# Block 1 of a fused attention and SwiGLU kernel: t's weight blocks made ahead of the weights' own, the last two pairs' steps moved into the down phase, silu queued behind the copy of P7

## The chip, the core and the metric

The kernel runs on one core of a Trainium2 chip. The metric is device time in microseconds (us), the median of several executions. A core has five engines with a queue of their own each, and each works through its queue in order: PE (TensorE, matrix products; PEld is its weight load), DVE (VectorE), ACT (ScalarE), POOL (GpSimd), and SP (SyncE), which here only issues DMA transfers. PE writes into PSUM banks; DVE and ACT read them and write SBUF; POOL works on SBUF alone.

## The reference

All in float32: linear attention with an RMS norm for 8 batches of 576 tokens and 8 heads of 64, then a SwiGLU feed-forward over 4608 tokens of width 512 with an inner width of 1536.

```python
kv = np.einsum('bhsd,bhse->bhde', k, v)
out = np.einsum('bhsd,bhde->bhse', q, kv)
rms = np.sqrt(np.mean(out * out, axis=-1, keepdims=True) + 1e-06)
x = (out / rms * g_norm)            # -> (4608, 512)
...
g = x @ w_gate
silu = g * (1.0 / (1.0 + np.exp(-g)))
val = x @ w_val
return silu * val @ w_out
```

## The kernel before

The 4608 tokens are nine blocks of 512, `blocks[0]` to `blocks[8]`. For each block n an `Ffn` object runs an *up* phase (gate and value products, silu, their product into the tile h) and a *down* phase (h times w_out). While block n is in its down phase, the attention of block n+1 is done in between: `Att.steps` gives three pieces of work that `down` runs after its products P1, P6 and P2 (query times kv and the norm of the first half; the same for the second half; the rest with `sums`).

Matrix products are done with seven block products in place of eight (Winograd's form of Strassen's method), named P1 to P7 by the number p in `multiply(p)`. Three PSUM banks carry the chains: b takes P1, P6, P7 and P4 one after the other; a takes P2; c takes P5 and then P3. After each product a method `after1` to `after7` takes what stands in the bank: ACT copies b after P1 (line 567), P6 (line 571) and P7 (line 601), DVE adds a after P2 (line 597) and c after P7 (line 603) and P3 (line 611). A product that adds to a bank must wait until the former contents have been read: P4 waits for the copy of P7, P3 for the add of c at line 603, P6 for the copy of P1. The DVE and POOL operations show in the profile with the lines of three helpers: add is L111, sub is L112, mul is L113.

Block 0 uses plain products. Block 1 uses one level of the seven-product form (class `Up`): six units, one for each pair j of 128-wide column groups; a unit holds pair j of w_gate and of w_val as a 2 x 2 block matrix. Blocks 2 to 8 (`DEEP` = 2) use two levels (class `Inner`), for which the second-level weight blocks, the *leaves*, have to exist. They are made once, in block 1, from the weights that its products have just used:

- For each unit, POOL makes three tiles t (for P5, P7 and P4) in `prepare`, one unit ahead, from a pool of nine.
- `leaf_steps` yields the making of leaves as small functions: for each operand two in-place steps on DVE, two more DVE subtractions into a room, and sends of the results to DRAM tiles w0 to w2 on SP's queue. For t's operands the room is a tile r and there are two sends (w<-t and w<-r). For the weights' own operands (o = 1, 2 in w_gate and 6, 3 in w_val) the room is the tile xi (`leaf_room`, one for all pairs), with one send (w<-xi) for w_gate and one for w_val; the rest stays in place.
- `Up.multiply` puts these steps into the list `making` after P5, P7 and P4 (t's) and after P3 (the weights' own); `make(4)` runs four after each product of the up phase, `make(12)` twelve after each of the down phase.

Unit i runs in the order P1, P5, then P4 and P3 of unit i-1, then P6, P2, P7 (`sequence`). P4 and P3 of a pair therefore lie in the next pair's unit. After P4, ACT applies silu to one half and POOL multiplies it into h (line 608); after P3 DVE adds c and POOL multiplies again (line 612), and DVE's `h_sums` reads and changes that part of h. After P7, before this change, ACT's queue holds the silu of s (line 602, on the sum that line 597 made on DVE) and then the copy of P7 (line 601).

The down phase of block 1 runs P1, P5, P6, P7, P2, P4, P3. Its t tiles are made by POOL from w_out (`turn_t`; t<-wo in the profile). Block 2 fetches its leaves from DRAM on SP's queue through the same nine t tiles (`Stream.pump`, t<-w in the profile), and its `sums` write a tile xi from the same single buffer as `leaf_room`. On SP, block 1 also holds loads of k and v (lines 263), of q for block 2 (line 300), and of q for block 3 in 32 small pieces (line 280).

A scheduler orders each engine's instructions at build time by the order in the program and by its own estimate of when each can start; `tc.issue_after(ins)` keeps what is traced inside it behind `ins` where both are on the same engine, without a wait of its own between engines.

Of the kernel before, what the change touches and what calls it, by code (L numbers as in the profile page):

```python
# [12 lines left out]
ACT = mybir.ActivationFunctionType  # L13
# [5 lines left out]
def kernel(  # L19
# [41 lines left out]
    nc = tc.nc  # L61
# [11 lines left out]
    NP = NF // 2  # L73
# [34 lines left out]
    wg, wv = ([consts.tile([P, NS, 2 * P], F32, name=f"{x}{j}") for j in range(NP)] for x in ("wg", "wv"))  # L108
# [6 lines left out]
    def ring():  # L115

        return r_pool.tile([P, 4, BLK], F32, name="r")

    class Words:
# [12 lines left out]
        def __init__(self, src, shape):  # L132
            self.raw = ld_pool.tile([P, LD], U32, name="ld")[:, 0 : 2 * BLK]
            dst = self.raw.rearrange("p (a b) -> p a b", a=shape[0])
            self.sent = nc.sync.dma_start(out=dst, in_=src)
            self.shape = shape
            self.begun = False
# [392 lines left out]
    class Quad:  # L530
# [11 lines left out]
        def multiply(self, p):  # L542
            name, first = CHAIN[p]
            if first:
                tiles = [PSUMS[name].tile([P, 2, HB], F32, name=name) for _ in range(1 + (name in self.apart))]
                self.ps[name], self.apart[name] = tiles[0], tiles[-1]
            banks = self.ps[name], self.apart[name]
            for e, i in self.order(p):
                lhsT, rhs = self.operands(p, e, i)

                nc.tensor.matmul(  # L551
                    banks[e][:, e], lhsT=lhsT, rhs=rhs, start=first and i == 0 and (e == 0 or banks[0] is not banks[1]),
                    stop=i == self.steps - 1, skip_group_check=True,
                )
            getattr(self, f"after{p}", lambda: None)()
# [17 lines left out]
    class Up(Quad):  # L573
# [24 lines left out]

        def after7(self):
            self.u3 = self.piece(2)  # L600
            nc.scalar.copy(out=self.u3, in_=self.ps["b"])
            nc.scalar.activation(out=self.s, in_=self.s, func=ACT.Silu)
            add(nc.vector, self.u3, self.ps["c"], self.u3)

        def after4(self):
# [9 lines left out]
        def multiply(self, p):  # L615
            super().multiply(p)
            ffn = self.ffn
            if ffn.n != DEEP - 1:
                return

            if p == 5:
                self.leaf_room = ring().rearrange("p f (s c) -> p (f s) c", c=P)
            if p in (5, 7, 4):
                at = 3 * (5, 7, 4).index(p)
                ffn.making.extend(leaf_steps(self.j, [(self.w[p].unsqueeze(1), (p,))], self.leaf_room[:, at:]))
            if p == 3:
                if ffn.leaf_room is None:
                    ffn.leaf_room = x_pool.tile([P, 3, 7, P], F32, name="xi").rearrange("p a b c -> p (a b) c")
                halves = lambda t: t[self.j].rearrange("p (o i) c -> p o i c", o=2)
                ffn.making.extend(leaf_steps(self.j, [(halves(wg), (1, 2)), (halves(wv), (6, 3))], ffn.leaf_room))  # L630

    class Inner:

# [167 lines left out]
    def leaf_steps(j, sources, room):  # L801


        d, f = divmod(j, 2)
        i = 0

        def send(leaf, count, src):
            at = LEAVES.index(leaf)
            tc.keep_in_program_order(nc.sync.dma_start(out=stream.dram[d][:, at : at + count, f], in_=src))

        for t, os in sources:
            n = len(os)
            t = t.rearrange("p o i (e c) -> p o i e c", e=2)
            b11, t2_, b22 = t[:, :, 0, 0], t[:, :, 0, 1], t[:, :, 1, 1]
            to = room[:, i : i + 3 * n].rearrange("p (o r) c -> p o r c", r=3)
            yield lambda b22=b22, t2_=t2_: sub(nc.vector, t2_, b22, t2_)
            yield lambda b11=b11, t2_=t2_: add(nc.vector, t2_, t2_, b11)
            yield lambda t=t, t2_=t2_, to=to, n=n: sub(
                nc.vector, to[:, :, 0:3:2], t[:, :, 1], t2_.unsqueeze(2).to_broadcast([P, n, 2, P])
            )  # L820
            if os[0] not in RESIDENT:
                yield lambda t=t, o=os[0]: send((o, 1), 4, t[:, 0].rearrange("p i e c -> p (i e) c"))
            yield lambda b11=b11, t2_=t2_, to=to: sub(nc.vector, to[:, :, 1], b11, t2_)
            yield lambda i=i, n=n, o=os[0]: send((o, 4), 3 * n, room[:, i : i + 3 * n])
            i += 3 * n
# [88 lines left out]
    class Ffn:  # L914
        def __init__(self, n, att):
            self.n, self.att = n, att
            self.h = h_pool.tile([P, NF, BLK], F32, name="h")
            self.ps, self.making, self.leaf_room, self.ended = {}, [], None, None

        def store(self, o, t, columns=slice(None)):  # L920
            rows = out[BLK * self.n : BLK * (self.n + 1), columns].rearrange("(t p) d -> p t d", t=T)
# [8 lines left out]
            return sub(engine, a21, s1, a11)  # L930

        def make(self, count):
            for step in self.making[0:count]:
                step()
            del self.making[0:count]

        def up(self, fill):

# [25 lines left out]
        def down(self, nxt):  # L964

            down = self.down_
            fill = nxt.steps() if nxt else {}
            for p in (1, 6, 5, 7, 2, 4, 3) if 5 in fill else (1, 5, 6, 7, 2, 4, 3):
                if p == 1:
                    down.turn_t(7, self.ended)  # L970
                if p == 6:
                    down.turn_t(4, nxt.halves[0] if nxt and nxt.n >= TURNED else None)
                down.multiply(p)
                self.make(12)
                if p == 5 and self.n == DEEP - 1:
                    for i in range(2):
                        self.loads(i)
                if p in fill:
                    fill[p]()
                if p == 1:  # L980
                    down.turn_s3()

# [59 lines left out]
    for n in range(NB):  # L1042
        ffn = Ffn(n, blocks[n])
        nxt = blocks[n + 1] if n + 1 < NB else None
        if n == 0:
# [4 lines left out]
            copied = blocks[0].copied  # L1050
# [78 lines left out]
```

## Time and profile before

| | us |
|---|---|
| runs | 1038.65, 1037.74, 1037.13, 1037.91; median 1037.83 |
| profiled execution | 1036.51 |
| its span, first to last instruction | 1034.7 |
| up phase of block 1, about | 158.8 to 241.5 |
| down phase of block 1, about | 242.6 to 283.6 |
| one product of a unit on PE (8 matmuls) | 1.73 from start to start |
| one product of the down phase (24 matmuls) | 5.2 |

The granted TensorE clock was 0.999 over the span. Group rows of the profile give line, engine, operation, out<-in with the names of tiles, shapes and count, then busy time, mean ns of one, and idle time of the engine just before with what ended it. These are the groups of the leaf steps and their sends, with durations as min, median and max:

| what | count | ns |
|---|---|---|
| t<-t on DVE, sub, 128x128 | 18 | 277 / 284 / 293 |
| r<-t on DVE, sub, two shapes | 36 | 277 / 416 / 1380 |
| wg<-wg on DVE, sub | 6 | 411 / 412 / 1239 |
| xi<-wg on DVE, sub, two shapes | 12 | 416 / 550 / 681 |
| xi<-wv on DVE, sub, two shapes | 12 | 410 / 553 / 1649 |
| copy of P7 on ACT, line 601 | 6 | 567 / 567 / 568 |

| sends and loads near block 1 | KB each | median us to landing |
|---|---|---|
| w<-t | 256 | 2.4 |
| w<-r | 192 | 2.2 |
| w<-xi | 384 | 3.0 |
| q of block 2 | 256 | 4.4 |
| t<-w | 256 | 3.5 |

### The profile page before, as it was taken

What the parts mean: (1) busy time and instruction counts of PE and PEld (TensorE: products, weight loads), DVE (VectorE), ACT (ScalarE), POOL (GpSimd) and SP (SyncE); (2) the same over time, 40 slices, a digit from 0 to 9 for tenths busy, and PEclk for the clock granted to TensorE, in tenths of its full rate; (3) what the DMA queues carried; (4) which work ended last, traced back from release to release, by engine and by line L of the source; (5) the groups of instructions that cost most, each with busy time, mean ns of one, the idle gap of its engine ahead of it and who ended that gap; (6) DMA issues with size and microseconds to landing.
All of it is one profiled execution on the core that took longest, in us unless ns stands there. A gap on an engine that the chain in (4) does not pass through costs nothing.

```text
span 1034.7 us, 21446 instructions
## 1 busy us (share of the span) xinstructions
PE 1014.2 (98%) x8586; PEld 904.6 (87%) x8586; DVE 700.2 (68%) x1184; ACT 231.5 (22%) x362; POOL 369.4 (36%) x280
## 2 busy tenths in 40 slices
PE   6999999999999999999999999999999999999998
PEld 4544788778899989998999899988999899989997
DVE  2999596898556856575666666674668466856661
ACT  2765121221212211212111112111212111211110
POOL 0000453335025622463156305640454136513670
PEclk9999999999999999999999999999999999999999
DMA  8689604775468456855686468736862766067601
GB/s 232 201 257 270 130 1 127 189 217 126 127 203 244 110 112 211 241 147 99 191 246 174 64 205 235 205 52 179 245 194 51 170 198 194 22 153 215 189 30 42
DMA packets 247876, 168.15 MB, mean 163 GB/s; under 512 B 124640, under 2 KB 215904, under 8 KB 247776
## 3 DMA queue, kind: packets, MB, share of 16 engines
q1 hardware_dynamic: 221280, 163.36, 57.0%
q10 hardware_dynamic: 26432, 3.41, 2.1%
q8 instruction: 68, 1.11, 0.4%
q14 instruction: 32, 0.26, 0.1%
q0 software_dynamic: 64, 0.00, 0.0%
HBM read 138.02 MB, written 22.41 MB: 155 GB/s over the span
## 4 chain that ended last, share of the span: by engine, by line
PE 91%; DVE 5%; DMA 2%; issue 1%; ACT 1%; SPq 0%; POOL 0%; DVEq 0%; ACTq 0%; POOLq 0%
PE b L700 25%; PE b L551 20%; PE c L700 13%; PE c L551 9%; PE a L700 6%; PE a L551 5%; PE b L994 4%; PE c L994 4%; PE m L316 2%; PE m L357 1%; DVE xi L112 1%; DVE r L112 1%; DMA h<-in_v_dram 1%; DVE r L111 0%; DVE h L112 0%
## 5 line engine op out<-in xcount | busy, mean ns | idle before, releaser
L111 POOL TENSOR_TENSOR r<-r 128x256 f32<-128x256 f32 (+1 forms) x105 | 110.9, 1062 | 308.5 <-DVE r L111 234.4
L111 DVE TENSOR_TENSOR r<-b,r 128x512 f32<-128x512 f32 (+1 forms) x273 | 162.0, 606 | 63.9 <-PE b L700 59.2
L112 POOL TENSOR_TENSOR t<-wo 128x512 f32<-128x512 f32 x81 | 115.4, 1452 | 190.4 <-DVE wo L111 103.9
L111 DVE TENSOR_TENSOR r<-c,r 128x512 f32<-128x512 f32 (+1 forms) x179 | 108.5, 617 | 95.5 <-PE c L700 56.1
L700 PE MATMUL b<-x,t 128*128 128x128 f32 x1092 | 151.0, 275 | 0.0
L700 PEld LDWEIGHTS b<-x,t 128*128 128x128 f32 x1092 | 136.5, 192 | 0.6
L111 DVE TENSOR_TENSOR r<-a,r 128x512 f32<-128x512 f32 (+1 forms) x99 | 62.5, 631 | 108.6 <-PE a L551 65.8
L113 POOL TENSOR_TENSOR h<-r 128x1024 f32<-128x1024 f32 (+1 forms) x40 | 81.9, 2063 | 88.3 <-DVE r L111 73.8
L700 PE MATMUL c<-xi,t 128*128 128x128 f32 x840 | 112.2, 275 | 0.4 <-DVE xi L111 0.4
L700 PEld LDWEIGHTS c<-xi,t 128*128 128x128 f32 x840 | 102.8, 192 | 0.5 <-DVE xi L111 0.5
L551 PE MATMUL b<-wo,h 128*128 128x256 f32 x432 | 99.4, 382 | 0.1
L551 PE MATMUL b<-t,h 128*128 128x256 f32 x432 | 96.9, 381 | 0.0
L551 PEld LDWEIGHTS b<-t,h 128*128 128x128 f32 x432 | 81.3, 190 | 11.3 <-issue 0.2
L551 PEld LDWEIGHTS b<-wo,h 128*128 128x128 f32 x432 | 79.9, 190 | 12.7 <-DVE h L113 2.5
L714 ACT COPY r<-b 128x512 f32<-128x512 f32 x63 | 36.9, 586 | 212.0 <-PE b L700 200.1
L700 PE MATMUL b<-xi,t 128*128 128x128 f32 x588 | 79.7, 276 | 0.0
L700 PEld LDWEIGHTS b<-xi,t 128*128 128x128 f32 x588 | 72.4, 192 | 0.0
L700 PE MATMUL b<-x,wg 128*128 128x128 f32 x336 | 52.7, 279 | 0.2 <-DVE x L112 0.2
L700 PE MATMUL b<-x,wv 128*128 128x128 f32 x336 | 51.3, 275 | 0.0
L551 PE MATMUL c<-t,s 128*128 128x256 f32 x216 | 48.3, 380 | 0.0
L551 PE MATMUL a<-wo,h 128*128 128x256 f32 x216 | 48.3, 379 | 0.0
L551 PE MATMUL c<-wo,h 128*128 128x256 f32 x216 | 48.1, 379 | 0.0
(136 smaller groups left out, 1578.0 us busy)
## 6 DMA issues: line engine op xcount, KB each, us to landing
t<-w SPq DMA_DIRECT2D x336, 256.0 KB, 3.5
out_dram<-r SPq DMA_DIRECT2D x17, 512.0 KB, 3.1
ld<-in_k_dram SPq DMA_DIRECT2D x26, 288.0 KB, 4.7
ld<-in_v_dram SPq DMA_DIRECT2D x26, 288.0 KB, 5.5
ld<-in_moe_w_gate_dram SPq DMA_DIRECT2D x12, 512.0 KB, 4.7
ld<-in_moe_w_val_dram SPq DMA_DIRECT2D x12, 512.0 KB, 4.6
ld<-in_moe_w_out_dram SPq DMA_DIRECT2D x12, 512.0 KB, 5.1
w<-t SPq DMA_DIRECT2D x18, 256.0 KB, 2.4
```

The costliest lines, as they stand in the source:

```text
L111: add = lambda e, o, a, b: e.tensor_tensor(out=o, in0=a, in1=b, op=OP.add)
L112: sub = lambda e, o, a, b: e.tensor_tensor(out=o, in0=a, in1=b, op=OP.subtract)
L113: mul = lambda e, o, a, b: e.tensor_tensor(out=o, in0=a, in1=b, op=OP.mult)
L316: nc.tensor.matmul(self.kv_ps[r][u * D : (u + 1) * D, g, :], lhsT=k[:, u, c, :], rhs=v[:, u, c, :], start=(c == 0), stop=(c == KT - 1),)
L357: self.multiplied = nc.tensor.matmul(self.ps[i][u][p : p + D, t, j, :], lhsT=self.qt[rows, 2 * i + t, j, p : p + D], rhs=kvs[b % 3][rows, ...
L551: nc.tensor.matmul(banks[e][:, e], lhsT=lhsT, rhs=rhs, start=first and i == 0 and (e == 0 or banks[0] is not banks[1]), stop=i == self.ste ...
L700: nc.tensor.matmul(ps[:, i, f], lhsT=self.weight(o, p, f), rhs=self.operand(o, p), start=first and (i, f) == (0, 0), stop=True, skip_group ...
L714: nc.scalar.copy(out=dst, in_=ps)
L994: nc.tensor.matmul(t, lhsT=w[f // 2][:, i, P * (f % 2) : P * (f % 2 + 1)], rhs=x[:, i, of], start=(i == 0), stop=(i == NS - 1),)
```

## The change

It touches block 1 alone, and there three things. In `Up.after7` the copy of P7 is issued first, and the silu is kept behind it on ACT. The weights' own leaf steps go into a second list `later`, which `make` takes from only when `making` (t's steps) is empty. For the last two pairs (j = 4, 5) they go into neither: they are kept as a bundle each in `latest`, and `down` runs the first bundle after P1's piece of the next block's attention, the second after P7, with DVE's part kept behind the last scaling of that norm half (`nxt.scaled`). No operation, transfer or buffer is added or removed.

```diff
         def after7(self):
             self.u3 = self.piece(2)
-            nc.scalar.copy(out=self.u3, in_=self.ps["b"])
-            nc.scalar.activation(out=self.s, in_=self.s, func=ACT.Silu)
+            copied = nc.scalar.copy(out=self.u3, in_=self.ps["b"])
+
+            with tc.issue_after(copied.ins):
+                nc.scalar.activation(out=self.s, in_=self.s, func=ACT.Silu)
             add(nc.vector, self.u3, self.ps["c"], self.u3)
...
-                ffn.making.extend(leaf_steps(self.j, [(halves(wg), (1, 2)), (halves(wv), (6, 3))], ffn.leaf_room))
+                steps = leaf_steps(self.j, [(halves(wg), (1, 2)), (halves(wv), (6, 3))], ffn.leaf_room)
+                if self.j < NP - 2:
+                    ffn.later.extend(steps)
+                else:
+                    ffn.latest.append(steps)
...
         def make(self, count):
-            for step in self.making[0:count]:
-                step()
-            del self.making[0:count]
+            for _ in range(count):
+                steps = self.making or self.later
+                if steps:
+                    steps.pop(0)()
...
                 if p in fill:
                     fill[p]()
+                if p in (1, 7) and self.latest:
+
+                    with tc.issue_after(nxt.scaled.ins):
+                        for step in self.latest.pop(0):
+                            step()
                 if p == 1:
                     down.turn_s3()
```

More of the change, by code (lines that the diff above doesn't have):

```diff
@@ L917, in __init__ @@
             self.h = h_pool.tile([P, NF, BLK], F32, name="h")
-            self.ps, self.making, self.leaf_room, self.ended = {}, [], None, None
+            self.ps, self.leaf_room, self.ended = {}, None, None
+            self.making, self.later, self.latest = [], [], []
         def store(self, o, t, columns=slice(None)):
```

## The prediction

> **What bounds the kernel now.** I read the page first, then PE's own waits and its timeline for block 1, then DVE, POOL and the sync queue beside it. The page says that PE sets the time, with DVE in second place on the chain:
>
> ```profile
> PE 1014.2 (98%) x8586; PEld 904.6 (87%) x8586; DVE 700.2 (68%) x1184; ACT 231.5 (22%) x362; POOL 369.4 (36%) x280
> ...
> PE 91%; DVE 5%; DMA 2%; issue 1%; ACT 1%; SPq 0%; POOL 0%; DVEq 0%; ACTq 0%; POOLq 0%
> ```
>
> So only time in which PE stands still can be won. In block 1 (up phase 158.8 to 241.5 us, down phase 242.6 to 283.6) the waits name one place:
>
> ```profile
> PE b L551 <- ACT r L601: 5.7, 4, 2.4
> ```
>
> ```profile
> 158.80:241.50 82.70, 77.05 (x488) 66.30 (x487) 73.02 (x145) 17.18 (x32) 30.40 (x23) 1.00 0.63 176
> 193.00:239.80 46.80, 41.15 (x256) 34.92 (x256) 44.48 (x89) 9.76 (x19) 17.86 (x14) 1.00 0.69 194
> 242.60:283.60 41.00, 41.00 (x314) 35.97 (x313) 27.50 (x48) 7.95 (x15) 10.37 (x7) 1.00 0.47 121
> ```
>
> Columns of the stretches: length, then busy time of PE, PEld, DVE, ACT, POOL. PE is idle 5.65 us in the up phase and not at all in the down phase; DVE is busy 44.5 of 46.8 us in the middle row and 27.5 of 41 in the last. PE's timeline shows three of the four idle times (the fourth, 1.69 us, is before 237.97):
>
> ```profile
> 199.06 1.99 PE L551 MATMUL b<-x,t 128*128 128x256 f32 x8 [2.41 <-ACT r L601]
> ...
> 213.42 1.99 PE L551 MATMUL b<-x,t 128*128 128x256 f32 x8 [0.60 <-ACT r L601]
> ...
> 226.73 1.99 PE L551 MATMUL b<-x,t 128*128 128x256 f32 x8 [0.95 <-ACT r L601]
> ```
>
> These are P4 of pairs 2, 3, 4 (then 5), each run inside the next pair's unit. From start to start they lose 2.57, 0.76, 1.12 and 1.85 us, together 6.3. P4 accumulates in the bank that line 601 copies; line 601 stands on ACT behind the silu of line 602, and that waits for DVE's add of P2 (line 597; call it A). DVE is late. The chain that ended last shows why:
>
> ```profile
> 187.95 4.02 DMA w<-t
> 192.13 1.12 POOL t L112
> 193.36 1.28 POOL h L113
> 194.66 1.47 DVE h L112
> ```
>
> A t tile is sent to DRAM, POOL waits for that landing to refill the tile, its product for h is queued behind, and DVE waits for h. From 194.66 DVE has no idle time until after 231.
>
> **The change, part by part.** I compared the order in which the two built programs issue. PE's order is the same. ACT has line 601 ahead of the silu in all six units. DVE's order is the same up to pair 3: making t's blocks first changes nothing there, since the scheduler had already interleaved them so; for pairs 4 and 5 the weights' own steps leave the up phase. They are per pair 8 DVE operations and 2 sends (384 KB, xi to DRAM), so 16 and 4 in all. On POOL one product for h (pair 3, after P3) moves behind a t<-wo. On SP an xi send changes place with a q load, or with a k or v load.
>
> *Silu behind the copy.* Line 601 then runs at P7's end plus 0.59 us, and P4 no longer waits. But P3, which follows 1.73 us later, accumulates in the bank that DVE's add of line 603 (call it C) must have read, and C starts on DVE 1.9 us behind A (197.19 and 199.12, 211.54 and 213.48) whatever ACT does. So the wait passes from P4 to P3 and shrinks. Behind the silu is the next P1's copy (line 567), wanted by P6: pair 2's silu ends at 198.0 and that copy at 198.5, P6 starts at 201.1; the other pairs have more.
>
> Pair 2: P4 at 194.76 + 1.73 = 196.49, P3 could start at 198.22. C ended at 199.12 + 0.68 = 199.80. The POOL wait above may end sooner: ahead of that send stood three q loads, and now two and an xi send. Median landings are 4.4 us (q) and 3.0 (xi), so 0 to 1.4 us; I take 0.5, a good third, as the xi send still takes its turn. C ends at 199.3, P3 starts at 199.35 instead of 200.89.
>
> Pair 3: without a stall P3 would follow at 199.35 + (215.25 - 200.89 - 0.76) = 212.95. DVE has no idle time from 194.66 on, so C keeps its distance: 214.16 - 0.5 = 213.66. P3 at 213.7 (before 215.25).
>
> Pair 4: PE could start P3 at 213.7 + (228.56 - 215.25 - 1.12) = 225.9. Here the weights' steps are gone from DVE, but POOL's swap enters. Rows of before:
>
> ```profile
> 217.20 0.53 SPq L809 DMA_DIRECT2D w<-t  x1
> ```
>
> ```profile
> 220.45 1.38 POOL L113 TENSOR_TENSOR h<-r 128x512 f32<-128x512 f32 x1 [1.83 <-DVE r L111]
> 222.26 1.26 POOL L112 TENSOR_TENSOR t<-wo 128x512 f32<-128x512 f32 x1 [0.43 <-DMA w<-t]
> ```
>
> The t<-wo waits for the send issued at 217.20; the product at 220.45 now stands behind it, and DVE's subtraction into h (222.30 before) behind that. The send follows the r send (214.73 - 0.5), an xi send (0.4 to issue) and two k loads (0.65 each), so it issues at 216.3; three loads were ahead of it before. POOL began 5.1 us after the issue then (222.26); one load less and one xi more leave it at 5.1, so 221.4. Bounds: 2.4 us, the median of such sends (218.7), and 7.3, the longest of any send or fetch of this stream (223.6). Then t<-wo to 222.8, the product to 224.2, and on DVE the h subtraction and the xi subtraction (0.35 each to the next start), A at 225.0, four t steps (1.2), C 226.85 to 227.55. P3 at 227.6 (before 228.56).
>
> Pair 5: 227.6 + (239.77 - 228.56 - 1.85) = 236.96. The only late thing here is line 601, at P7's end plus 0.6, 0.1 us behind the transposes that PE does in between. C comes at 236.6, in time: DVE has lost the steps that stood in its way, and fits two POOL products (1.4 us each) meanwhile. P3 at 237.05 instead of 239.77: 2.7 us won.
>
> *The down phase.* Pair 4's eight operations stand behind the first half of the norm (DVE free at 258.0, idle 4.66 us before 262.69), pair 5's behind the second (267.6, idle 0.36 and 3.87 us up to 272.59, with one add for the output between). One pair takes 2 x (0.41 + 0.42 + 0.68 + 0.42) = 3.9 us busy, about 3.5 from start to end, as neighbours overlap: it fits both gaps. Without that cover the second set would meet line 885's subtraction, which P3 needs 3.5 us after it ended (274.95 against 278.45). POOL has nothing from 254.94 to 294.63, so nothing should stretch them. On SP pair 4's two sends stand inside the q loads of block 3: SP waits about from 254 for DVE until 260 to 261.7, and the first three stream fetches go at 267.5 instead of 263.4; landed by 271 to 273, they are wanted at 283.6. Pair 5's sends (270.4, 271.7) hold two fetches back until then, wanted after 287. The last send lands by 275 (3.2 us, as its equals took), the sums write that buffer from 277.6 on. The q loads are wanted a block later. Cost 0; bounds 0 and 6 us (the slower rival below).
>
> The Trainium skill, "SBUF — State Buffer", section "SBUF: two separate sides", says that VectorE with two SBUF inputs and GpSimd lock each other out for a whole instruction. The xi subtraction at 220.73 took 1.64 us beside POOL's product, and 0.68 elsewhere. By that rule one POOL instruction can hold up one DVE instruction, so with POOL idle the eight cost 3.5 us and the down phase 0; by the stretched row alone it would be the rival's 13.
>
> Sum: 2.57 + 0.76 + 1.12 + 1.85 = 6.3 removed, 1.13 + 0.75 + 1.7 + 0.1 = 3.7 returned as waits of P3 (and 0.1 for a line 601), net near 2.7. The profiled execution took 1036.51 us (span 1034.7 and 1.8 around it), 1.3 below the median of the runs, 1037.83. I expect a span of 1032.0 and a median of 1037.83 - 2.7 = 1035.1. By the bounds of the two landings the gain lies between 4.4 (the pair 4 send lands at once, P3 at 225.9) and about 1.9 (no 0.5 us won, send freed at 222.1).
>
> **Rivals.** (1) All four stalls go: 1037.8 - 6.3 = 1031.5. For it: the four waits name line 601 alone. Against: C's rows (199.12, 213.48) come after P3's free start. (2) POOL's swap eats the gain: the tile is freed at 222.5 to 224.5, each us later makes P3 of pair 4 one later, and 0 to 1.5 us are left: about 1036.8. For it: sends in this stretch took up to 5.0 us, and the queue ahead is as long as before. Against: one load less. (3) Slower: the second set of eight meets another engine on SBUF. At the stretched price 8 x 1.64 = 13.1 us from 268.3 end at 281.4, the add of P2 (0.6) and line 885's subtraction (1.75) at 283.8, and P3 of the down phase waits 5.4 us: 1035.1 + 5.4 = 1040.5. P3 begins to wait when the eight take over 7.8 us, and the gain is used up at 10.5. For it: DVE shows such rows beside POOL. Against: POOL's empty stretch.
>
> **How the numbers follow.** The forecast has 0.65, rival 1 0.08, rival 2 0.19, rival 3 0.08. A difference within 0.2% (2.1 us) can't be told from none: faster 0.65 + 0.08 = 0.73, same 0.19, slower 0.08. The range leaves out rivals 1 and 3 (0.16): from 1037.8 - 4.4, 1033.3, to the near end of rival 2, 1037.0; the forecast's own is 1033.4 to 1035.9.
>
> **What would show it.** In the profile after: no wait of P4 on ACT above 0.2 us; P3 of pairs 2, 3, 4 waits for DVE's add of r<-c, about 1.1, 0.8, 1.7 us, the last with DVE idle about 3 us for POOL's h; PE without a wait in block 1's down phase; xi steps of pairs 4 and 5 at 0.68 us after each norm half. I am wrong if P3 doesn't wait, if POOL's t<-wo of pair 3 starts after 223, or if PE waits for h or xi late in the down phase.

## The result, and the profile after

| | before | after |
|---|---|---|
| median | 1037.80 us (54 runs, 1036.20 to 1039.66) | 1036.22 us (36 runs, 1034.69 to 1037.36) |
| ratio | | 0.9984, 95% interval 0.9979 to 0.9989 |
| profiled execution (span) | 1036.51 (1034.7) | 1035.93 (1034.2) |
| block 1 begins | 158.82 | 159.89 |
| its up phase | 83.77 | 81.11 |
| block 1, up to the first product of block 2 | 124.81 | 122.15 |

The change takes 1.6 us off the median (1.1 to 2.2 by the interval). In the two profiles block 1 became 2.66 us shorter. It began 1.07 us later, though, after a stretch in which the two programs are the same; in what follows, times of after are compared from block 1's start.

The page of after, engine totals and the shares of the chain that ended last:

```profile
PE 1014.9 (98%) x8586; PEld 905.2 (88%) x8586; DVE 695.3 (67%) x1184; ACT 231.6 (22%) x362; POOL 368.8 (36%) x280
...
PE 91%; DVE 4%; DMA 2%; issue 1%; ACT 1%; POOL 0%; SPq 0%; DVEq 0%; POOLq 0%; ACTq 0%
```

PE still sets the time. PE's waits in after from 140 to 300 us (total, times, longest), and the same three stretches as before (length, then busy time of PE, PEld, DVE, ACT, POOL):

```profile
PE c L551 <- DVE r L111: 2.8, 2, 1.7
```

```profile
158.80:241.50 82.70, 79.71 (x505) 68.78 (x504) 66.27 (x135) 18.45 (x35) 30.61 (x24) 1.00 0.63 172
193.00:239.80 46.80, 43.81 (x268) 37.27 (x267) 37.80 (x81) 10.47 (x20) 19.23 (x15) 1.00 0.72 199
242.60:283.60 41.00, 41.00 (x320) 36.12 (x319) 30.68 (x60) 7.37 (x13) 9.09 (x7) 1.00 0.51 133
```

The wait of bank b on ACT's copy is gone from the list. In its place bank c waits for DVE. PE's idle time in the first row fell from 5.65 to 2.99 us; DVE's work in the middle row fell from 44.5 to 37.8 us, and rose in the down phase from 27.5 to 30.7, where PE stays busy for all 41 us.

PE's timeline after, P3 of pairs 2, 3 and 4:

```profile
201.13 1.99 PE L551 MATMUL c<-x,wv 128*128 128x256 f32 x8 [1.68 <-DVE r L111]
...
214.94 1.99 PE L551 MATMUL c<-x,wv 128*128 128x256 f32 x8
...
228.44 1.99 PE L551 MATMUL c<-x,wv 128*128 128x256 f32 x8 [1.15 <-DVE r L111]
```

P3 of pair 2 waits 1.68 us and that of pair 4 1.15 us, each for the add of line 603 (C in the prediction). For the second one, POOL's and DVE's timelines of after:

```profile
222.71 1.27 POOL L112 TENSOR_TENSOR t<-wo 128x512 f32<-128x512 f32 x1 [3.35 <-DMA w<-t]
223.94 1.26 POOL L113 TENSOR_TENSOR h<-r 128x512 f32<-128x512 f32 x1
```

```profile
225.24 0.42 DVE L112 TENSOR_TENSOR h<-s,h 128x256 f32<-128x256 f32 x1 [3.06 <-POOL h L113]
...
227.70 0.68 DVE L111 TENSOR_TENSOR r<-c,r 128x512 f32<-128x512 f32 x1
```

This is the swap on POOL: the tile t<-wo waits 3.35 us for a send, pair 3's product for h stands behind it, DVE is idle 3.06 us for that product, and so C (227.70) is late for P3 (228.44).

In the down phase, DVE's timeline after has the two bundles where they were meant to be. Of pair 4's, the last four steps and what follows; of pair 5's, the end and what follows:

```profile
256.85 1.02 DVE L112 TENSOR_TENSOR xi<-wg 128x512 f32<-128x512 f32 x2
257.79 1.02 DVE L112 TENSOR_TENSOR xi<-wv 128x512 f32<-128x512 f32 x2
261.10 1.28 DVE L369 TENSOR_REDUCE z<-r 128x8 f32<-128x512 f32 x2 [2.29 <-ACT r L368]
...
268.99 1.03 DVE L112 TENSOR_TENSOR xi<-wv 128x512 f32<-128x512 f32 x2
271.00 0.69 DVE L111 TENSOR_TENSOR r<-a,r 128x512 f32<-128x512 f32 x1 [0.99 <-PE a L551]
```

Each row of two steps is 1.02 us, none is stretched, and DVE is idle again behind each bundle (2.29 and 0.99 us).

P3 is the product that ends each pair, so its start is the best mark. In us from the start of block 1's first product, worked out from PE's timeline of each profile (the prediction's times less 158.82):

| P3 of pair | before | predicted | after | after, a second profile |
|---|---|---|---|---|
| 2 | 42.07 | 40.53 | 41.24 | 41.24 |
| 3 | 56.43 | 54.88 | 55.05 | 55.65 |
| 4 | 69.74 | 68.78 | 68.55 | 69.16 |
| 5 | 80.95 | 78.23 | 78.29 | 78.90 |

### The profile page after: what moved, and what is told of

Same layout as the page of the kernel before. It is cut to its first block, busy times and chain, and to the rows that moved or that the text cites. A ratio compares the mean times of both kernels' runs of the same rounds, so it can differ in the third digit from the quotient of the medians.

```text
span 1034.2 us, 21447 instructions
## 1 busy us (share of the span) xinstructions
PE 1014.9 (98%) x8586; PEld 905.2 (88%) x8586; DVE 695.3 (67%) x1184; ACT 231.6 (22%) x362; POOL 368.8 (36%) x280
## 4 chain that ended last, share of the span: by engine, by line
PE 91%; DVE 4%; DMA 2%; issue 1%; ACT 1%; POOL 0%; SPq 0%; DVEq 0%; POOLq 0%; ACTq 0%
PE b L706 26%; PE b L551 20%; PE c L706 13%; PE c L551 10%; PE a L706 6%; PE a L551 5%; PE b L1008 4%; PE c L1008 4%; PE m L316 1%; PE m L357 1%; DMA h<-in_v_dram 1%; DVE xi L112 1%; DVE r L112 1%; DVE r L111 1%; DMA w<-t 1%
```

## The experiments

The theory was the prediction's: silu behind the copy passes the wait from P4 to P3, the bundles take load off DVE, and POOL's swap gives part of it back. Rivals were that one part alone brings the gain, that the swap costs nothing, and that the later start of block 1 belongs to the change.

**The two kernels again, unchanged** (c_before, c_after).

> The kernel before, unchanged, once more, for a second profile. The changed kernel gained 2.66 us inside block 1 in its profile (from block 1's first product to block 2's first: 124.81 us before, 122.15 after), but only 1.6 us in the medians, and its profile began block 1 1.07 us later, from waits for loads in the first 21 us, where the two programs are the same. Theory A (chance: those waits vary from one execution to the next): block 1 again takes 124.8 us here within 0.3, its start lies anywhere between 158.3 and 160.2 us, and the ratio is 1.000. Theory B (the change makes the start later in every execution): the start is 158.8 within 0.3 here.

> The changed kernel, unchanged, once more. Theory A: block 1 takes 122.15 us within 0.4 and starts anywhere between 158.3 and 160.2 us. Theory B: it starts at 159.9 within 0.3 again. Theory C (about 1 us is lost after block 1 in every execution, as one wait of PE for a stream fetch near 717 us in the first profile hints): from block 2's first product to the end it takes 0.8 us more than in the kernel before. Ratio 0.9984 as before.

Measured: c_before 1.0004 [0.9995, 1.0013], block 1 124.97 us; c_after 0.9983 [0.9974, 0.9991], block 1 122.75. The gain of after is there again. In this profile it is 2.2 us of block 1, not 2.66: P3 of pair 3 is 0.6 us later than in the first profile of the same program, and all behind it too. DVE's and POOL's timelines show why. First after, DVE and POOL:

```profile
206.29 0.42 DVE L112 TENSOR_TENSOR wv<-wv 128x256 f32<-128x256 f32 x1
206.63 0.68 DVE L111 TENSOR_TENSOR r<-c,r 128x512 f32<-128x512 f32 x1
```

```profile
206.27 1.57 POOL L112 TENSOR_TENSOR t<-wg,wv 128x512 f32<-128x512 f32 x1 [0.72 <-PE a L551]
```

Then the same instructions in c_after:

```profile
205.83 1.50 DVE L112 TENSOR_TENSOR wv<-wv 128x256 f32<-128x256 f32 x1
207.25 0.68 DVE L111 TENSOR_TENSOR r<-c,r 128x512 f32<-128x512 f32 x1
```

```profile
205.78 1.27 POOL L112 TENSOR_TENSOR t<-wg,wv 128x512 f32<-128x512 f32 x1 [0.70 <-PE a L551]
```

DVE's row begins 20 ns behind POOL's in after and 50 ns behind it in c_after. In after POOL's row is the longer one (1.57 for 1.27 us), in c_after DVE's (1.50 for 0.42), and then the add behind it comes 1.1 us later, P3 of pair 3 0.6 us later.

This race is in seven of the profiles kept. In four (after and, of the runs below, e_pool, e_pool2 and e_turn) DVE's row begins 20 to 30 ns behind POOL's and POOL's is the long one; in three (c_after, e_move and e_later) it begins 40 to 50 ns behind and DVE's is the long one. Two profiles can be compared to better than 0.6 us only where the race went the same way in both. The kernel before and e_silu have no such pair of rows: there POOL's tile starts 1.9 us ahead of that DVE row, beside two subtractions of DVE that take 2.65 us together (1.58 in after and c_after). DVE is thus held up there as well, and only a race that DVE wins is a gain on them.

**Silu behind the copy alone** (e_silu): the kernel before with only this.

```diff
+            copied = nc.scalar.copy(out=self.u3, in_=self.ps["b"])
+            with tc.issue_after(copied.ins):
+                nc.scalar.activation(out=self.s, in_=self.s, func=ACT.Silu)
-            nc.scalar.copy(out=self.u3, in_=self.ps["b"])
-            nc.scalar.activation(out=self.s, in_=self.s, func=ACT.Silu)
```

> Only the silu behind the copy of P7; all else, DVE's order too, as before. My theory (P3 then waits for DVE's add of c, which is late): P4 waits for nothing, P3 of pairs 2, 3, 4 and 5 starts at the end of that add, and 0.5 us (0 to 1.0) are won in block 1: 124.3 us, ratio 0.9995. The rival (line 601 alone was the wait): 6.3 us are won, 118.5 us, ratio 0.994.

Measured: 1.0003 [0.9994, 1.0011], block 1 124.55 us. PE's waits from 140 to 300 us:

```profile
PE c L551 <- DVE r L111: 5.0, 4, 2.0
```

The wait has passed from P4 to P3 in all four pairs. P3 of pairs 2, 3 and 4 start at 41.07, 55.44 and 68.73, a full 1.0 us sooner than before, as C allows; P3 of pair 5 starts at 80.59, only 0.36 sooner, for C of that pair ends at 80.54 (80.40 before). DVE still has the weights' own steps of every pair to do there and has no idle time to make up, so most of what the first three pairs win is lost at the last.

**The rest of the change without it** (e_move): after, with the silu ahead of the copy again (the reverse of the diff above).

> Only the leaf steps moved (the second list and the two bundles in the down phase); silu ahead of the copy as before. My theory: P4 of pairs 2, 3 and 4 waits on ACT as before (2.4, 0.6, 0.95 us; for pair 4 DVE waits for POOL's product instead of having the steps to do), P4 of pair 5 no longer; 1.7 us are won in block 1: 123.1 us, ratio 0.9984. If the parts were independent of each other, this would win 2.66 - 0.5 = 2.2. Rival (the silu does all): 0 won, 124.8.

Measured: 0.9994 [0.9985, 1.0003], block 1 123.80 us, 1.0 less than before. PE's waits from 140 to 300 us:

```profile
PE b L551 <- ACT r L601: 4.5, 3, 2.6
```

DVE has room for pair 5 now, but P4 of the three pairs before waits for ACT as it did before. The forecast was 1.7 us won, and 0.7 of it are missing; in this profile the race of c_after went against DVE (1.50 us for 0.42), which can account for up to 0.6. So the two parts help each other: 0.3 and 1.0 us alone, 2.1 together with the race as in e_move (c_after) and 2.7 with it the other way. This is read from one profile of each part; the intervals of the two medians alone (up to 0.6 and 1.6 us won) would not show it.

**No bundles** (e_later, one execution): all of the weights' own steps go into the second list.

```diff
-                if self.j < NP - 2:
+                if self.j < NP:
```

> The changed kernel without the bundles: all pairs' own steps go into the second list, none into the down phase; silu behind the copy. My theory (making t's blocks first changes nothing of DVE's order up to pair 4): as the silu alone, block 1 in 124.55 us within 0.4. Rival (t's blocks first help by themselves): 123.5 or less.

Measured: 1039.86 us in one execution, block 1 126.76 us: 2.2 worse than e_silu, not equal to it as the theory had it. DVE issues the same as in e_silu but for one xi step. POOL does not: making t's steps first has the scheduler put t<-wo ahead of pair 3's product, without any bundle. (SP's queue differs too: xi sends change places with loads, as in after.) POOL's and DVE's timelines:

```profile
223.93 1.26 POOL L112 TENSOR_TENSOR t<-wo 128x512 f32<-128x512 f32 x1 [3.58 <-DMA w<-t]
225.15 1.27 POOL L113 TENSOR_TENSOR h<-r 128x512 f32<-128x512 f32 x1
```

```profile
226.46 0.42 DVE L112 TENSOR_TENSOR h<-s,h 128x256 f32<-128x256 f32 x1 [3.29 <-POOL h L113]
```

Here DVE stands idle 3.29 us in a stretch where it has too much to do. So "t's blocks first" by itself costs about 2.2 us in this one profile. The bundles are worth about 4.0 (126.76 against 122.75 in c_after, where the race went the same way).

**POOL's swap undone** (e_pool, and once more as e_pool2): after, with that t<-wo held behind pair 3's product. The products are kept in a list in `after3`; no other engine's order changes.

```diff
+                with ExitStack() as held:
+                    if p == 5 and i == 4 and self.ffn.products:
+                        held.enter_context(tc.issue_after(self.ffn.products[3].ins))
-                turned = sub(nc.gpsimd, t, of[:, i : i + 2], pairs[:, 0, i : i + 2, HD:DM])
+                    turned = sub(nc.gpsimd, t, of[:, i : i + 2], pairs[:, 0, i : i + 2, HD:DM])
```

> The changed kernel, with the third t<-wo of P5 held behind pair 3's second product for h on POOL, as it stood before the change. My theory (for pair 4 DVE stands still for 3.06 us behind that product, then P3 waits 1.15): DVE's idle time before the h subtraction of pair 3 is under 0.5 us, P3 of pair 4 starts 0.7 us sooner (it is then bound by DVE's own work), block 1 takes 121.7 us against 122.45, the mean of the two profiles of the changed kernel; ratio 0.9977. Rival (DVE's work is the bound there, the product is not): 122.45, no change.

> The changed kernel with POOL's third t<-wo held behind the second product of pair 3, once more. If its gain is real: ratio 0.995 to 0.9975, block 1 near 121.0 us, one wait of P3 (pair 2, 1.6 us). If the first figure was lucky: block 1 122 or more, ratio 0.998.

Measured: 0.9962 [0.9949, 0.9976] and 0.9972 [0.9961, 0.9984]; block 1 120.98 and 121.01 us. POOL's and DVE's timelines of e_pool2:

```profile
220.31 1.38 POOL L113 TENSOR_TENSOR h<-r 128x512 f32<-128x512 f32 x1 [1.83 <-DVE r L111]
221.81 1.54 POOL L112 TENSOR_TENSOR t<-wo 128x512 f32<-128x512 f32 x1
```

```profile
220.59 1.64 DVE L112 TENSOR_TENSOR xi<-wv 128x512 f32<-128x512 f32 x1
222.16 1.48 DVE L112 TENSOR_TENSOR h<-s,h 128x256 f32<-128x256 f32 x1
...
225.68 0.68 DVE L111 TENSOR_TENSOR r<-c,r 128x512 f32<-128x512 f32 x1
```

The product runs as soon as DVE's add is there, and DVE has no idle time; two rows beside POOL are stretched (1.64 for 0.69, 1.48 for 0.42), yet C ends at 67.32 and 67.35 from the start in place of 68.50. The swap cost about 1.15 us: 122.15 in the first profile of after less 121.0, all three with the race of pair 3 the same way (P3 of pair 3 at 55.05, 55.00 and 55.04). Against 122.45, the mean of the two profiles of after, it would be 1.45, but 0.3 of that is the race. The forecast for e_pool had 0.75; rows and both medians give more.

**The weights' own steps held behind C** (e_dve), and **both** (e_both): the steps of pairs 0 to 3 are issued on DVE behind line 603's add.

```diff
-                    ffn.later.extend(steps)
+                    ffn.later.extend(self.held(step) for step in steps)
```

> The changed kernel, with the own steps of pairs 0 to 3 held on DVE behind the add of c that follows P7 (call it C), so that only t's steps stand between the add of P2 and C. My theory: P3 of pair 2 waits 0.6 us in place of 1.7, P3 of pair 3 not at all, but pair 4's P3 still waits for C, which stands behind DVE's wait for POOL's product: its start does not move, the wait there grows to about 2.8, and block 1 stays at 122.45 within 0.4. Rival (the own steps ahead of C are what costs): 1.9 us won, 120.5.

> Both of the foregoing edits. My theory: P3 of pair 4 is then bound by DVE's work alone; about 1.0 us more than the changed kernel wins, 121.4 us in block 1, ratio 0.9974. If the two waits add up (each hides the other): 119.9 us, ratio 0.996.

Measured: e_dve 0.9971 [0.9961, 0.9982], block 1 121.82 us; e_both 0.9982 [0.9973, 0.9991], 122.30. Both miss what was expected, in opposite directions. P3 of pair 2 comes at 40.46 in both, 0.8 us sooner than in after. But the held steps now stand between C and the add that follows P3: that add ends at 62.37 and 62.52 us from the start, 61.2 in e_pool. In e_dve that add is still sooner than POOL's product, which stands behind t<-wo and runs at 63.1. In e_both the product is ahead of t<-wo and waits for the add instead (POOL's timeline of e_both; 1.3 us later from the start than in e_pool):

```profile
222.14 1.37 POOL L113 TENSOR_TENSOR h<-r 128x512 f32<-128x512 f32 x1 [3.67 <-DVE r L111]
```

So the two edits don't add up: each moves the late thing into the other's way. (The medians of the two overlap in their intervals; the order of the two is read from one profile each.)

**The same cure for pair 2** (e_turn): e_pool, and the third tile t of pair 4 held behind pair 1's product in the same manner.

```diff
+                with ExitStack() as held:
+                    if j == 4 and b is b21:
+                        held.enter_context(tc.issue_after(self.ffn.products[1].ins))
-                sub(nc.gpsimd, t[-1], b, t2)
+                    sub(nc.gpsimd, t[-1], b, t2)
```

> As e_pool2, and POOL's third tile t of pair 4 held behind the second product of pair 1, the same cure at the second place. No other engine's order changes. If P3 of pair 2 waits only because that product stands behind a tile that waits for its send (193.3 us), the product runs near 192.5, DVE's subtraction into h near 193.7 in place of 195.9, and P3's wait of 1.6 us goes: block 1 near 119.4, ratio near 0.9945. If DVE has no room there anyway, or its rows beside POOL stretch, P3 keeps 0.8 us or more of its wait: block 1 120.2 to 121.5.

Measured: 0.9959 [0.9946, 0.9971], median 1033.57 us beside 1037.97 for before; block 1 120.03 us. This is the fastest kernel of the study, though its interval overlaps e_pool2's. POOL's and DVE's timelines:

```profile
191.04 1.38 POOL L113 TENSOR_TENSOR h<-r 128x512 f32<-128x512 f32 x1 [1.83 <-DVE r L111]
```

```profile
191.32 1.64 DVE L112 TENSOR_TENSOR xi<-wv 128x512 f32<-128x512 f32 x1
192.89 1.49 DVE L112 TENSOR_TENSOR h<-s,h 128x256 f32<-128x256 f32 x1
194.30 1.49 DVE L112 TENSOR_TENSOR xi<-wv 128x256 f32<-128x256 f32 x1
```

The product comes early and the 2.9 us of idle DVE time are gone. But three rows are long here, where in e_pool only one of them was (1.64, 1.49, 1.49 against 0.69, 1.47, 0.41), and P3 of pair 2 keeps 0.73 us of its wait. The cure brings 1.0 of the 1.6 us: between the two theories.

**The start of block 1** (n_before, m_before: the kernel before, one execution each).

> The kernel before, unchanged, one look. Two profiles of it so far began block 1 at 158.82 and 159.02 us; eight profiles of the other kernels, whose programs are the same up to there, at 159.43 to 160.71. Chance: the start lies anywhere from 158.8 to 160.7. A difference that belongs to the changed program: the start lies at 158.8 to 159.1 again. Block 1 near 124.9 us.

> The kernel before, unchanged, a further look, for the start of block 1 as in n_before: 158.8 to 160.7 by chance, 158.8 to 159.1 if the start belongs to the program.

Measured: start 160.35 and 159.74 us, block 1 124.71 and 124.80, times 1038.46 and 1037.06 us. With 158.82 and 159.02 for the same program earlier, and 158.89 for e_turn, the start is chance. The 1.07 us by which after began later is no part of the change.

## Why the prediction came out as it did

The forecast was 1035.1 us with 1033.3 to 1037.0; measured were 1036.2. The time lies in the range, 1.1 us above the forecast and outside the forecast's own 1033.4 to 1035.9. The gain of 1.6 us is real by its interval, but it is below the 2.1 us that the prediction named as its bound for "faster": by that bound it is the "same" that had a chance of 0.19.

- *The wait passes from P4 to P3, and shrinks.* Right: e_silu shows it alone, and the waits of after name bank c and DVE's add only.
- *Pair 2, "I take 0.5".* This term failed. It was to make POOL's tile 0.5 us sooner and P3 1.13 us later than PE could start it; P3 starts 1.84 us later than that (1.68 of it idle). The sync queue's rows, before and then after:

```profile
185.70 2.14 SPq L300 DMA_DIRECT2D ld<-in_q_dram  x3
187.95 0.89 SPq L809 DMA_DIRECT2D w<-t  x1
```

```profile
186.75 0.49 SPq L815 DMA_DIRECT2D w<-xi  x1
187.33 1.65 SPq L300 DMA_DIRECT2D ld<-in_q_dram  x2
189.09 1.23 SPq L815 DMA_DIRECT2D w<-t  x1
```

The send issues at 29.13 us from block 1's start before and 29.20 after, and on the chain of after it takes about as long (before: 4.02 us):

```profile
189.09 4.16 DMA w<-t
```

POOL's tile waits for that landing (POOL's timeline of after):

```profile
193.41 1.27 POOL L112 TENSOR_TENSOR t<-wg,wv 128x512 f32<-128x512 f32 x1 [3.19 <-DMA w<-t]
```

The tile is refilled at 33.52 (before 33.31): 0.2 us later, 0.7 from the forecast. The sum had priced a place in the queue by the difference of the landings (4.4 and 3.0 us). The queue goes on to the next transfer long before a landing: three loads took it 2.25 us (185.70 to 187.95), the xi send and two loads 2.34 (186.75 to 189.09).
- *Pair 3.* 54.88 was forecast, 55.05 and 55.65 were seen. The step "C keeps its distance" to pair 2's C holds in c_after (14.41 us, 14.36 before), where the 0.7 us missed at pair 2 are still missing and P3 starts 0.8 us later than PE could, as forecast (0.75). In the first profile of after the race between the two rows 20 to 50 ns apart cut the distance to 13.81 us and gave 0.6 back, and that start is only 0.2 us late. No term of the sum had this: the near hit of the first profile is luck.
- *Pair 4, POOL's swap.* Right in kind and about right in size: t<-wo forecast at 62.58 from the start, seen at 62.82 and 63.44; DVE idle about 3 us, seen 3.06; P3 at 68.78, seen 68.55 and 69.16. Two small errors cancel in the first profile: the send left at 58.10 in place of 57.5, and POOL began 4.7 us after it in place of 5.1.
- *Pair 5.* Right: nothing is late, P3 keeps its distance to that of pair 4.
- *Sum for block 1.* 2.7 forecast, 2.66 in the first profile, which agrees by the luck at pair 3. Over four profiles of before (124.82 on average) and two of after (122.45) it is 2.4, and in c_after alone 2.1, which is the forecast less what pair 2 missed.
- *The down phase at 0.* Right: PE 41.00 of 41.00 us, and no stretched row in the bundles. Rival 3 needed eight rows of 1.64 us beside another engine; POOL was empty there.
- *Nothing behind block 1.* Not quite. Leaving out the waits of 0.2 to 0.8 us for a fetched leaf, which show in single profiles of before, after and e_move alike, the time from block 2's first product to PE's end is 747.3 to 747.4 us in every kernel without bundles and 747.65 to 747.85 in every one with them. Those 0.3 us lie in the blocks that begin near 608 and 824 us (before), about 0.1 us at each of three products; the order on every engine is the same there. Their cause was not found.

2.4 less 0.3 is 2.1, near the upper end of the median's interval (1.1 to 2.2); with the race as in c_after it is 1.8, near the median itself. How often the race goes either way isn't known. Rival 1 is out, since P3 did wait. Rival 2 (1036.8) named a time nearer than the forecast did, but its condition wasn't met: the tile was to be freed 63.7 us or later from the start, and was refilled at 62.8 and 63.4. Its mechanism, the swap, was in the sum and did cost about 1.15 us; a hold on one instruction takes it out again, as e_pool shows.

The rule of the Trainium skill, "SBUF — State Buffer", section "SBUF: two separate sides", that VectorE with two SBUF inputs and a GpSimd instruction that reads SBUF lock each other out for a whole instruction, agrees with the two pairs of rows of after and c_after: one of the two engines ran its plain length, the other longer by 0.30 (POOL) or 1.08 us (DVE). Which of the two goes ahead can't be told from which row begins first: POOL's does in both.

## What to carry to other kernels

When a wait is moved from one product to the next, look at the engine behind the new wait: silu's place won 0.3 us of block 1 while DVE was full, and emptying DVE won 1.0 while the copy stood behind the silu. Compare the order on every queue, not only on the one that is edited: a list that reorders DVE's steps made the scheduler put a waiting tile ahead of a product on POOL, and one hold there was worth about 1.15 us in block 1 against the change's own 2.4. Price a place in a DMA queue by the queue's own rows, not by landings: a send whose landing took 1.4 us less than a load's freed nothing on the queue. Before two single profiles are compared, see whether a race between two engines went the same way in both.

## What was not expected of the hardware

- The same program gave 122.15 and 122.75 us for block 1, by which of two rows 20 to 50 ns apart, one on DVE and one on POOL, held the other up (0.42 to 1.50 us on DVE, 1.27 to 1.57 on POOL). In seven profiles DVE was held up where its row began 40 to 50 ns behind POOL's, and POOL where it was 20 to 30 ns.
- The first product of block 1 started anywhere from 158.82 to 160.71 us in 14 profiles, with the same instructions ahead of it; in four of the kernel before alone, from 158.82 to 160.35.
- Work that reaches DVE earlier isn't done earlier by as much: with POOL beside it a 128x512 subtraction took 1.64 us for 0.69, a 128x256 one 1.49 for 0.41, so that filling 2.9 us of idle time on DVE moved C of that pair by only 0.9 us.
